# A fused attention and channel-mix kernel: the same tasks in another order and on other engines, with two planner prices changed

## The chip, the cores and the metric

The kernel runs on one core of one Trainium2 chip. A core has a tensor engine (PE in the profile; its weight loads are shown as PEld), a vector engine (DVE), a scalar engine (ACT), GpSimd (POOL) and a sync engine (SP), which here only issues DMAs. The metric is the device time of one execution in microseconds (us), lower is better. The kernel before took 271.17 us as the median of 4 runs (269.69 to 272.12).

## The reference, cut to what matters

Eight batches, eight heads, 576 positions, head size 64. Attention is causal by blocks of 64 positions, its output becomes a matrix of 576 rows by 512 columns for each batch, and this goes through a channel-mix layer with a shift by one position.

```python
mask = (pos[:, None] // 64) >= (pos[None, :] // 64)
attn = softmax(where(mask, q @ k.T / 8, -1e9))           # 8 batches x 8 heads, 576 x 576
x = (attn @ v) as (8, 576, 512)                          # heads side by side
x_prev = x shifted by one position, zeros in front       # inside each batch
xk = mu_k * x + (1 - mu_k) * x_prev                      # and xr with mu_r
k = relu(xk @ w_k)                                       # 512 -> 1024
out = sigmoid(xr @ w_r) * ((k * k) @ w_v)                # 1024 -> 512
```

## The kernel before

**Work and its units.** The kernel computes batch after batch of attention and feeds the result, as columns of a transposed `x`, into ten chunks of the channel mix: chunks 0 and 1 have 256 positions, chunks 2 to 9 have 512. Chunk c (2 to 8) begins in the columns of batch c - 2 and ends in those of batch c - 1, chunk 9 lies in batch 7; the two halves of the kernel overlap, one batch's attention with an earlier chunk's channel mix.

Everything is cut into tasks. Those on PE have names, which the string `TENSOR` lists in the order in which PE executes them:

- `qBPN`: transposes of queries or keys of head pair P (only batches 0 and 1; later batches use a transposing DMA, L534);
- `sBPI` (and `sBtQ`): scores of batch B, pair P, part I (L652, L660). An exponential on ACT (`ex`, L679) follows, and on POOL a memset of masked corners (`zero`, L688);
- `dBQ` (for batch 0 also `eBQ`): the softmax sums of half Q of the heads (L725), followed on DVE by reciprocals (L777, L780) and shuffles that spread them (L786);
- `vBQI`: probabilities times values (L725), followed on DVE by the **normalization** (`norm`, L822, L833 and L835): it multiplies the sums in PSUM by the spread reciprocals and writes `x` (tile `t_xt`). In L833 and L835 the operands are read in steps of four positions, since the scores are laid out by residues of 4;
- `kCJ`: chunk C, column block J of the first matrix (L958), followed on ACT by relu (L969) and by a square `sqCJ` on ACT (L976), or on DVE or POOL (L978);
- `rCJ`: the gate matrix (L993), followed by tanh on ACT (L1004);
- `pCJ`: the projection back (L1024, 8 matmuls), followed on DVE by the product with the gate (`ov`, L1036) and on SP by the output DMA (L1042);
- fills (L1062), two matmuls each without use, put in where PE would stand idle before the first `k`.

Between the normalization and `kCJ` stand, for each of four column blocks cc of a chunk: the difference `dCcc` on DVE or POOL (L907), and two `mul` on DVE (L920) that make `xk` and `xr`; where a batch begins inside a chunk, a small `fix` on POOL (L935) for each of the two. So `kC0` waits for the last `norm`, the last difference, four `mul` of `xk` and the `fix`.

**What sets the order.** Nothing is scheduled at run time. `Plan` is given the order on PE (`TENSOR`) and for 260 further tasks the engine (`WHERE`: casts of loaded tensors `qk`, `v`, `wk`, `wr`, `wv`, evacuations `ev`, squares `sq`, differences `d`). Each task has a price in microseconds. From the prices `dues` derives when each task off PE is due, and `order` goes through a planned time and takes on each engine the most urgent task whose inputs and buffers are free by the plan. What comes out is a fixed sequence for each engine. On the chip each engine executes its sequence in order and waits where an input is late, with all that stands behind it. SP issues its DMAs in order too: the loads, the transposing DMAs and the outputs are one queue. A price does not change an instruction; it changes the sequences.

The sequences also depend on ring buffers (`RINGS`): 4 PSUM buffers `mm` for all matmul outputs but scores, 2 PSUM buffers `s` for scores, 4 tiles `e` of probabilities, 9 load buffers `ld`, and so on.

Of the kernel before, what the change touches and what calls it, by code (L numbers as in the profile page):

```python
# [21 lines left out]


TENSOR = """
q000 q010 q001 q011 s000 q030 s010 s001 q110 q100 q020 s011 s012 s002 s0t0 d00
v000 q021 q031 e00 s020 s0t1 q130 s030 s032 v001 s022 v002 q120 s021 s031 q131
q111 q121 q101 v010 d01 s110 s100 s1t0 s112 v011 e01 v012 s1t1 s102 k00 s111
s101 s130 k03 s120 d10 k10 s132 s131 k14 k16 k02 k01 k12 s121 s122 v100 k05
k07 v101 k13 k17 k11 k04 k06 d11 v102 r00 v111 r10 r01 k15 s200 s202 v112 v110
s2t0 r11 s210 s212 p00 p01 p10 p11 r21 r23 k20 k26 k27 k24 r20 k25 k22 s211  # L30
s201 k21 k23 r22 s230 d20 s220 p23 s221 v201 s232 v200 s231 v202 s222 p20 s2t1
v210 s300 d21 s301 s302 v211 s310 p21 v212 s312 s3t0 p22 s311 s330 k30 k31 k37
s331 s332 k32 r33 d30 s320 k34 s322 k35 r32 s321 s3t1 k33 r31 k36 d31 v300
v312 p32 r30 v311 p33 v301 v302 v310 s400 s401 p31 s402 s410 p30 s411 s4t0 k40
k44 s412 s430 k45 r42 r41 k43 d40 s431 k46 r43 s420 s421 k47 k42 k41 r40 v400
v401 v402 s432 s422 p40 s4t1 p43 d41 v411 v410 s500 p41 p42 v412 s501 s502 k50
k53 s510 s5t0 k57 k56 s512 k52 k51 k54 s520 s511 r53 r51 s530 s532 d50 r52 k55
s5t1 v500 v501 r50 s531 s522 p51 v502 s521 s600 p52 d51 s602 s601 v512 v511
v510 p50 p53 s610 s612 k60 k65 s620 s611 k62 r60 r62 s6t0 s630 k66 k63 k64 d60
s632 s631 k61 k67 s622 r63 v600 v601 v602 s6t1 r61 s621 p60 p61 s700 s702 d61  # L40
v611 v610 v612 s701 s710 p63 s730 s731 p62 s711 s712 k70 k74 k77 s7t0 s732 k73
k72 r73 k76 r70 s7t1 s720 d70 v700 v701 s721 s722 k71 r71 k75 r72 v702 d71
v711 v710 p72 p71 p73 p70 v712 k80 k87 k86 k83 k82 r80 k84 k85 r83 k81 r82 r81
p80 p83 p82 p81 r90 k90 k92 k91 k96 k93 k94 k97 k95 r93 r92 p90 r91 p91 p92
p93b p93a
"""


WHERE = {
    "ACT": "ev000 ev001 ev011 ev021 ev030 ev101 ev111 ev120 ev121 ev130 qk0001 "  # L50
            "qk1011 qk220 qk221 qk230 qk231 qk301 qk310 qk320 qk321 qk400 qk401 "
            "qk521 qk530 qk531 qk611 qk621 qk630 qk631 qk711 qk720 qk721 qk730 "
            "qk731 sq02 sq04 sq07 sq12 sq14 sq15 sq23 sq31 sq32 sq35 sq36 sq40 "
            "sq42 sq43 sq45 sq50 sq52 sq55 sq66 sq71 sq75 sq80 sq81 sq84 sq86 "
            "sq87 sq91 sq93 sq96 v04 v11 v12 v14 v20 v21 v22 v23 v32 v40 v42 "
            "v43 v64 v70 v71 wk5 wr1 wv1 wv5 wv6 wv7",
    "DVE": "d00 d02 d13 d20 d21 d22 d30 d32 d33 d42 d51 d53 d62 d63 d71 d72 "
            "d73 d82 d83 d90 d91 d92 d93 ev010 ev020 ev031 ev100 ev110 ev131 "
            "qk0000 qk0101 qk0111 qk1000 qk1001 qk1101 qk200 qk210 qk211 qk311 "
            "qk330 qk331 qk410 qk411 qk431 qk600 qk601 qk700 qk701 qk710 sq00 "  # L60
            "sq03 sq13 sq20 sq24 sq26 sq27 sq33 sq44 sq47 sq51 sq53 sq60 sq61 "
            "sq62 sq70 sq73 sq77 sq82 sq83 sq85 sq94 sq95 sq97 v00 v01 v02 v24 "
            "v30 v33 v41 v50 v54 wk3 wk6 wk7 wr2 wv0 wv3",
    "POOL": "d01 d03 d10 d11 d12 d23 d31 d40 d41 d43 d50 d52 d60 d61 d70 d80 "
            "d81 qk0010 qk0011 qk0100 qk0110 qk1010 qk1100 qk1110 qk1111 qk201 "
            "qk300 qk420 qk421 qk430 qk500 qk501 qk510 qk511 qk520 qk610 qk620 "
            "sq01 sq05 sq06 sq10 sq11 sq16 sq17 sq21 sq22 sq25 sq30 sq34 sq37 "
            "sq41 sq46 sq54 sq56 sq57 sq63 sq64 sq65 sq67 sq72 sq74 sq76 sq90 "
            "sq92 v03 v10 v13 v31 v34 v44 v51 v52 v53 v60 v61 v62 v63 v72 v73 "
            "v74 wk0 wk1 wk2 wk4 wr0 wr3 wv2 wv4",  # L70
}


# [207 lines left out]
def kernel(  # L281
# [24 lines left out]
    M = CUT // J  # L306
# [73 lines left out]
    def flex(key, alts, fn, deps, takes=(), uses=(), lock=BOTH):  # L380


        eng = ENGINE.get(key, next(iter(alts)))
        t = plan.add(eng, alts[eng], lambda: fn(eng), deps, takes, uses,
                     lock=lock)
        t["key"], t["alts"] = key, alts
        return t
# [324 lines left out]
    def add_values(b, Q):  # L712
# [98 lines left out]
        def scale(t, i, xs, a, z, c, first, lo, hi, buf, rd, spr, key):  # L811
            home = HOME[c]
            take = not xt_parts[home]
            off = lo - CHUNKS[home][0]
            ch = slice(2 * Q + xs[0], 2 * Q + xs[-1] + 1)

            def norm():
                x = xt_tile(c)[:, ch, 1 + off:1 + off + hi - lo]
                num, r = tiles["num", b, Q, i], tiles["rd", key]
                n = len(xs)  # L820
                if a == M:
                    nc.vector.tensor_tensor(  # L822
                        x, num[:, 0:n * D].rearrange("p (s t) -> p s t", s=n),
                        r[:, J * MP:].unsqueeze(1).to_broadcast([P, n, D]),
                        ALU.mult)
                    return
                p0, p1 = (lo - b * S) // J, (hi - b * S) // J
                num = num[:, 0:n * J * (z - a)].rearrange(
                    "q (s j p) -> q s p j", s=n, j=J)[:, :, p0 - a:p1 - a]
                r = r[:, 0:J * MP].rearrange("q (j p) -> q p j", j=J)[:, p0:p1]  # L830
                x = x.rearrange("q s (p j) -> q s p j", j=J)
                if n == 1:
                    nc.vector.tensor_tensor(x[:, 0], num[:, 0], r, ALU.mult)  # L833
                else:
                    nc.vector.tensor_tensor(  # L835
                        x, num, r.unsqueeze(1).to_broadcast(
                            [P, n, p1 - p0, J]), ALU.mult)
            dur = 0.2 if a == M else 0.00105 * (hi - lo) * len(xs) + 0.065
            xb = xtbuf[home]
            n = on("DVE", dur, norm, [t, spr], takes=[xb] if take else [],  # L840
                   uses=[buf, rd] + ([] if take else [xb]))
            xt_parts[c].append(n)
            for x in xs:
                xt_of[c].setdefault(2 * Q + x, []).append(n)
# [17 lines left out]
    def xt_tile(c):  # L862
        c = HOME[c]
        if ("xt", c) not in tiles:
            tiles["xt", c] = new("xt", [P, CCn, CH + 1], FP)
            if c == 0:
                nc.vector.memset(tiles["xt", c][:, :, 0:1], 0.0)
        return tiles["xt", c]
# [22 lines left out]
    def add_mix(c, cc):  # L891
# [7 lines left out]
        f = W[c] / CH  # L899
# [4 lines left out]
        def fn(eng):  # L904
# [5 lines left out]
        sub = flex(f"d{c}{cc}", {usual: alts[usual], **alts}, fn,  # L910
                   list(xt_of[c][cc]), takes=[d], uses=[xtbuf[h]])
        for n in range(2):
            name = ("xk", "xr")[n]
            buf = tiles[name + "b", h]
            first = cc == 0 and h == c

            def mul(n=n, name=name, first=first):
                if first:
                    tiles[name, c] = new(name, [P, CCn, CH], F16)
                nc.vector.scalar_tensor_tensor(  # L920
                    tiles[name, h][:, cc, o:o + w], tiles["d", c, cc][:, 0:w],
                    (MUK1, MUR1)[n][:, cc:cc + 1],
                    xt_tile(c)[:, cc, o + 1:o + w + 1], ALU.mult, ALU.add)
            mixed[c, n].append(on(
                "DVE", 0.12 + 0.545 * f, mul, [sub] + mu_ready,
                takes=[buf] if first else [],
                uses=[d, xtbuf[h]] + ([] if first else [buf]), lock=BOTH))
            if cc < CCn - 1:
                continue

            for b in range(B):
                at = b * S - CHUNKS[c][0]
                if 0 < at < w:
                    def fix(n=n, at=at, name=name):
                        nc.gpsimd.tensor_tensor(  # L935
                            tiles[name, h][:, :, at:at + 1],
                            xt_tile(c)[:, :, at + 1:at + 2],
                            (MUK, MUR)[n][:, :].unsqueeze(2), ALU.mult)
                    mixed[c, n].append(on(
                        "POOL", 0.16, fix, list(mixed[c, n]),  # L940
                        uses=[buf, xtbuf[h]], lock=BOTH))
# [105 lines left out]
    mu_ready = []  # L1047
# [87 lines left out]
```

## Time and profile before

| | before |
|---|---|
| median of 4 runs | 271.17 us (269.69 to 272.12) |
| the profiled execution | 270.27 us |
| its span, first to last instruction | 268.5 us |
| PE busy | 250.1 us (93%) |
| DVE busy | 204.7 us (76%) |
| ACT busy | 197.3 us (73%) |
| POOL busy | 116.2 us (43%) |
| mean granted PE clock | 0.992 of full speed |
| `norm`, 128x448 (L833), 8 of them | mean 934 ns |
| `mul`, 128x512 (L920), 64 of them | mean 809 and 813 ns |
| difference 128x512 (L907) | DVE 712 ns, POOL 1075 ns |

The profiled execution is one run, on which all rows and stages below rest; its own time is 270.27 us, 0.9 us under the median. A busy share says how long an engine had an instruction in it. On DVE and ACT an instruction begins some 0.08 to 0.1 us before the one ahead of it ends, so that the mean duration in a row is more than what one more instruction costs; where this matters, the distance from start to start is used. First `k` of chunk c (L958) stood at 36.0, 40.7, 68.1, 97.0, 123.1, 150.2, 178.0, 206.1, 230.7 and 248.8 us for c = 0 to 9, and the first projection `p00` at 59.4 us.

### The profile page before, as it was taken

To read this page: it belongs to the slowest core of one execution; us is meant where nothing else is said; L and a number is where in the kernel's file an instruction comes from. 1 tells how busy PE (TensorE), PEld (TensorE's weight loads), DVE (VectorE), ACT (ScalarE), POOL (GpSimd) and SP (SyncE) were. 2 spreads that over 40 slices of the span, in tenths; PEclk is the share of its full clock that TensorE was granted. 3 is DMA by queue.
4 is the path that set the end of the run, shared out by engine and by line. 5 is a ranking of instruction groups with operands and counts; after the bars stand their busy time and mean duration, and the time that the engine had idled before them with its cause. 6 is when DMAs were issued, how large, how long until landed. Compare 5 with 4: busy or idle time off the path is not lost.

```text
span 268.5 us, 9965 instructions
## 1 busy us (share of the span) xinstructions
PE 250.1 (93%) x4120; PEld 131.0 (49%) x4120; DVE 204.7 (76%) x477; ACT 197.3 (73%) x313; POOL 116.2 (43%) x265
## 2 busy tenths in 40 slices
PE   0999799999999699999999899999999999999995
PEld 0667456654445344544455354534453455444443
DVE  2579987999529984799379938996799599996033
ACT  2769979996898679669992799759978880490740
POOL 3337737954054245644572396527652640000300
PEclk9999889999999999999999999999999999999999
DMA  7999899999998999999999999999994101302113
GB/s 226 305 275 248 241 276 291 251 218 224 249 200 236 180 186 244 262 190 234 276 223 209 185 310 183 166 202 301 228 187 130 59 2 42 120 0 96 64 39 117
DMA packets 118302, 51.51 MB, mean 192 GB/s; under 512 B 102769, under 2 KB 109169, under 8 KB 118257
## 3 DMA queue, kind: packets, MB, share of 16 engines
q1 hardware_dynamic: 118256, 50.88, 86.0%
q8 instruction: 32, 0.52, 0.8%
q14 instruction: 14, 0.11, 0.1%
HBM read 33.56 MB, written 9.44 MB: 160 GB/s over the span
## 4 chain that ended last, share of the span: by engine, by line
PE 69%; DVE 13%; ACT 9%; DMA 5%; issue 2%; SPq 0%; POOL 0%; DVEq 0%; ACTq 0%
PE t_mm L958 23%; PE t_mm L1024 16%; PE t_mm L993 12%; PE t_mm L725 10%; ACT t_e L679 7%; PE t_s L652 6%; DVE t_xt L833 3%; DMA t_qkt<-NB 3%; DVE t_xk L920 2%; PE t_s L660 2%; DMA t_ld<-in_k_dram 2%; DVE t_d L907 2%; DVE t_rd L786 2%; DVE t_c L777 1%; DVE t_o L1036 1%
## 5 line engine op out<-in xcount | busy, mean ns | idle before, releaser
L679 ACT ACTIVATE t_e<-t_s 128x1024 f16<-128x1024 f32 x96 | 95.6, 1032 | 23.4 <-PE t_s L652 12.8
L958 PE MATMUL t_mm<-t_xk,WK 128*128 128x512 f16 (+1 forms) x320 | 68.9, 359 | 2.8 <-DVE t_xt L833 1.7
L1024 PE MATMUL t_mm<-WV,t_k 128*128 128x512 f16 (+1 forms) x296 | 66.0, 374 | 0.0
L969 ACT ACTIVATE t_kr<-t_mm 128x512 f32<-128x512 f32 (+1 forms) x80 | 43.9, 576 | 13.3 <-PE t_mm L958 13.0
L688 POOL MEMSET t_e<- 64x128 f16 x128 | 24.4, 208 | 57.0 <-ACT t_e L679 54.8
L958 PEld LDWEIGHTS <-WK 128*128 128x128 f16 x320 | 29.0, 98 | 33.5 <-issue 3.6
L1024 PEld LDWEIGHTS <-t_k 128*128 128x128 f16 x296 | 27.4, 98 | 31.8 <-issue 2.4
L652 PE MATMUL t_s<-t_qkt 64*128 64x128 bf16 (+3 forms) x272 | 35.9, 326 | 4.9 <-DMA t_qkt<-NB 2.9
L978 POOL TENSOR_TENSOR t_k<-t_kr 128x512 f16<-128x512 f32 (+1 forms) x27 | 26.2, 977 | 28.5 <-ACT t_kr L969 28.4
L993 PE MATMUL t_mm<-WR,t_xr 128*128 128x512 f16 x144 | 35.9, 380 | 0.0
L833 DVE TENSOR_TENSOR t_xt<-t_mm,t_rd 128x448 f32<-128x448 f32 (+6 forms) x56 | 30.7, 595 | 4.4 <-PE t_mm L725 4.0
L1004 ACT ACTIVATE t_t<-t_mm 128x512 f32<-128x512 f32 x36 | 21.8, 615 | 14.5 <-PE t_mm L993 14.3
L777 DVE RECIPROCAL t_c<-t_mm 128x128 f32<-128x128 f32 (+1 forms) x18 | 15.6, 865 | 20.8 <-PE t_mm L725 20.7
L1036 DVE SCALAR_TENSOR_TENSOR t_o<-t_t,t_mm 128x512 f32<-128x512 f32 (+1 forms) x37 | 24.4, 668 | 8.5 <-PE t_mm L1024 7.9
L920 DVE SCALAR_TENSOR_TENSOR t_xk<-t_d,MUK,t_xt 128x512 f16<-128x512 f32 (+1 forms) x40 | 29.5, 764 | 1.0 <-POOL t_d L907 0.9
L725 PE MATMUL t_mm<-t_e,VO 128*32 128x64 f16 (+4 forms) x1056 | 29.5, 252 | 0.2 <-DVE t_qkt L398 0.2
L920 DVE SCALAR_TENSOR_TENSOR t_xr<-t_d,MUR,t_xt 128x512 f16<-128x512 f32 (+1 forms) x40 | 29.2, 757 | 0.0
L978 DVE TENSOR_TENSOR t_k<-t_kr 128x512 f16<-128x512 f32 (+1 forms) x24 | 17.0, 723 | 15.4 <-ACT t_kr L969 15.1
L725 PEld LDWEIGHTS <-VO 128*32 128x32 f16 x1184 | 19.6, 99 | 10.6 <-issue 4.1
L660 PE MATMUL t_s<-t_qkt 64*128 64x64 bf16 x320 | 23.9, 197 | 0.6 <-ACT t_e L679 0.5
L652 PEld LDWEIGHTS <-t_qkt 64*128 64x128 bf16 x272 | 13.3, 96 | 17.5 <-issue 8.9
L993 PEld LDWEIGHTS <-t_xr 128*128 128x128 f16 x144 | 13.4, 98 | 16.1 <-issue 0.5
(61 smaller groups left out, 281.7 us busy)
## 6 DMA issues: line engine op xcount, KB each, us to landing
out_dram<-t_o SPq DMA_DIRECT2D x35, 256.0 KB, 3.5
t_vl<-in_v_dram SPq DMA_DIRECT2D x32, 256.0 KB, 5.6
t_ld<-in_k_dram SPq DMA_DIRECT2D x48, 128.0 KB, 4.2
t_ld<-in_q_dram SPq DMA_DIRECT2D x24, 256.0 KB, 4.1
t_ld<-in_q_dram SPq DMA_DIRECT2D x8, 288.0 KB, 5.7
t_ld<-in_k_dram SPq DMA_DIRECT2D x8, 288.0 KB, 5.1
t_ld<-in_moe_w_k_dram SPq DMA_DIRECT2D x8, 256.0 KB, 4.4
t_ld<-in_moe_w_v_dram SPq DMA_DIRECT2D x8, 256.0 KB, 3.9
```

The lines of the kernel that those rows point to most:

```text
L652: nc.tensor.matmul(PS[:, h, col:col + J * w].rearrange("p (j n) -> p j n", j=J), keys, ask[:, 0:CUT].rearrange("d (p j) -> d j p" if b < T ...
L660: nc.tensor.matmul(PS[:, h, col:col + D], keys, ask[:, CUT:S], start=True, stop=True)
L679: nc.scalar.activation(tiles["e", b, pr][:, :, i, :], tiles["ps", b, pr, i], AF.Exp, scale=ISQ)
L725: nc.tensor.matmul(ps[g * R:g * R + R], lhs, e, start=start, stop=stop, tile_position=(0, g * R))
L833: nc.vector.tensor_tensor(x[:, 0], num[:, 0], r, ALU.mult)
L920: nc.vector.scalar_tensor_tensor(tiles[name, h][:, cc, o:o + w], tiles["d", c, cc][:, 0:w], (MUK1, MUR1)[n][:, cc:cc + 1], xt_tile(c)[:, c ...
L958: nc.tensor.matmul(ps[:, 0:w], WK[:, cc, jc * P:(jc + 1) * P], tiles["xk", h][:, cc, o:o + w], start=(cc == 0), stop=(cc == CCn - 1))
L969: nc.scalar.activation(tiles["kr", c, jc][:, 0:w], tiles["pk", c, jc][:, 0:w], AF.Relu)
L978: (nc.vector if eng == "DVE" else nc.gpsimd).tensor_tensor(K2, KR, KR, ALU.mult)
L993: nc.tensor.matmul(ps, tiles["xr", h][:, cc, o + jt * P:o + (jt + 1) * P], WR[:, cc], start=(cc == 0), stop=(cc == CCn - 1))
L1024: nc.tensor.matmul(ps[:, 0:w], tiles["k2", h][:, jc, off:off + P], WV[:, jc, cols], start=(jc == 0), stop=(jc == JCn - 1))
L1036: nc.vector.scalar_tensor_tensor(tiles["o", c, jt, part][:, 0:w], tiles["t", c, jt][:, cols], 1.0, tiles["pv", c, jt, part][:, 0:w], ALU.a ...
```

## The change

Three things are replaced together.

1. Two prices in the planner. The normalization's price goes from 0.00105 to 0.00174 us for each column and head (plus 0.065 us), and the price of a `mul` from 0.12 + 0.545 f to 0.14 + 0.525 f, where f is the chunk's share of 512 columns (so 0.665 both before and after for a full chunk, and 0.3925 against 0.4025 for a half one).
2. `TENSOR`: the same task names in another order.
3. `WHERE`: 166 of 260 tasks go to another engine. By kind, before and after, as DVE / ACT / POOL: differences 23/0/17 and 16/0/24; squares 24/29/27 and 29/25/26; casts of queries and keys 20/24/20 and 18/24/22; casts of values 9/15/16 and 12/14/14; casts of the first matrix 3/1/4 and 1/2/5, of the gate matrix 1/1/2 and 0/2/2, of the last matrix 2/4/2 and 3/4/1; evacuations 6/10/0 both.

No other instruction is added or removed, but for the fills: the plan puts in 16 before and 12 after.

```diff
 TENSOR = """
-q000 q010 q001 q011 s000 q030 s010 s001 q110 q100 q020 s011 s012 s002 s0t0 d00
-v000 q021 q031 e00 s020 s0t1 q130 s030 s032 v001 s022 v002 q120 s021 s031 q131
-q111 q121 q101 v010 d01 s110 s100 s1t0 s112 v011 e01 v012 s1t1 s102 k00 s111
...
-r33 d30 s320 k34 s322 k35 r32 s321 s3t1 k33 r31 k36 d31 v300
-v312 p32 r30 v311 p33 v301 v302 v310 s400 s401 p31 s402 s410 p30 s411 s4t0 k40
...
-v400
-v401 v402 s432 s422 p40 s4t1 p43 d41 v411 v410 s500 p41 p42 v412 s501 s502 k50
-k53 s510 s5t0 k57 k56 s512 k52 k51 k54 s520 s511 r53 r51 s530 s532 d50 r52 k55
-s5t1 v500 v501 r50 s531 s522 p51 v502 s521 s600 p52 d51 s602 s601 v512 v511
-v510 p50 p53 s610 s612 k60
...
+q000 q001 q011 q010 s000 s010 q031 s001 s011 q020 q021 q030 d00 v000 s012 s030
+q100 q110 s002 s020 s0t0 s021 s032 d01 q101 v010 s0t1 e00 s031 v001 v002 s022
+s100 q111 s101 k00 k02 k01 s110 q120 s111 e01 v011 v012 q131 s112 s1t0 q130
...
+s3t1 p31 d31 s400 s402 p33 v312 v311 v310 p30 p32 s401 k40
...
+p41 s421 s422 p40 s4t1 v401 d41 s500 s501 p43 v411 v410 s5t0 s510 v412
+s512 s502 p42 s511 s530 k50
...
+r51 d51 v511 v510 s601 s602 v512
+p50 s610 s6t0 p51 p53 s620 s611 p52 s630 s612 k60
...
 WHERE = {
-    "DVE": "... d82 d83 d90 d91 d92 d93 ..."
+    "POOL": "... d80 d81 d82 d83 d90 d91 d92 d93 ..."
...
-            dur = 0.2 if a == M else 0.00105 * (hi - lo) * len(xs) + 0.065
+            dur = 0.2 if a == M else 0.00174 * (hi - lo) * len(xs) + 0.065
...
-                "DVE", 0.12 + 0.545 * f, mul, [sub] + mu_ready,
+                "DVE", 0.14 + 0.525 * f, mul, [sub] + mu_ready,
```

## The prediction

> **What bounds the kernel now.** I read the page's busy shares first, then stages, then what PE waited for, then the start-up on ACT.
>
> ```profile
> PE 250.1 (93%) x4120; PEld 131.0 (49%) x4120; DVE 204.7 (76%) x477; ACT 197.3 (73%) x313; POOL 116.2 (43%) x265
> ...
> PE 69%; DVE 13%; ACT 9%; DMA 5%; issue 2%; SPq 0%; POOL 0%; DVEq 0%; ACTq 0%
> ```
>
> The second line is the chain that ended last: 69% is PE, the rest is where PE stood behind DVE, ACT or a DMA. The change leaves PE's work as it is, so it can win back only such time. Stages (busy us of PE, PEld, DVE, ACT, POOL, each with its instructions, then clock, DMA share and GB/s):
>
> ```profile
> 10.00:40.00 30.00, 27.43 (x700) 18.90 (x699) 25.68 (x78) 24.73 (x34) 16.28 (x42) 0.94 0.99 261
> 68.00:97.00 29.00, 26.49 (x473) 12.95 (x471) 21.49 (x51) 23.80 (x36) 9.59 (x26) 1.00 1.06 215
> 150.00:178.00 28.00, 27.32 (x474) 13.44 (x474) 22.16 (x53) 22.70 (x35) 16.36 (x38) 1.00 1.18 217
> 230.60:268.50 37.90, 34.73 (x168) 16.38 (x168) 20.64 (x35) 17.76 (x32) 2.25 (x3) 0.99 0.20 77
> ```
>
> The middle runs at 98% of PE with about half a microsecond lost per chunk, the end at 100% but for the last output. PE's own waits, in us in total, times, longest:
>
> ```profile
> PE t_s L652 <- DMA t_qkt<-NB: 2.9, 2, 2.5
> PE t_mm L958 <- DVE t_xt L833: 1.7, 2, 1.2
> PE t_s L652 <- ACT t_e L679: 1.4, 3, 0.7
> PE t_mm L958 <- DVE t_o L1036: 0.4, 1, 0.4
> ```
>
> After 60 us PE's gaps are 2.51 (at 91.64, `s310` behind its transposing DMA), 1.22 (150.19, `k50`), 0.52 (178.03, `k60`), 0.36 (203.03, a DMA again) and 0.39 (230.67, `k80`): **5.0 us** that an order can remove. Before 60 us ACT sets the pace; its idle times there are in brackets:
>
> ```profile
> 18.82 0.64 ACT L392 COPY t_qkt<-t_mm 128x576 bf16<-128x576 bf16 x1 [1.27 <-PE t_mm L470]
> 20.77 1.02 ACT L679 ACTIVATE t_e<-t_s 128x1024 f16<-128x1024 f32 x1 [1.31 <-PE t_s L660]
> 35.67 0.38 ACT L667 ACTIVATE EL<-t_s 64x256 f16<-64x256 f32 x1 [1.58 <-PE t_s L660]
> ```
>
> That is **4.2 us** of idle time of the engine that sets the pace.
>
> **Is the new price right?** Four normalizations in a row on DVE, 448, 64, 448 and 64 columns:
>
> ```profile
> 217.35 2.14 DVE L833 TENSOR_TENSOR t_xt<-t_mm,t_rd 128x448 f32<-128x448 f32 x4
> ```
>
> The old price gives 2 x (0.535 + 0.132) = 1.33 us, the new one 2 x (0.845 + 0.176) = 2.04. The old plan therefore saw 0.00069 x 2048 = 1.4 us too little DVE work for each batch (512 columns, 2 halves, 2 heads, twice). It is missing on the way from a chunk's last `dB1` to its `kC0`, and it shows in who releases PE: not the `mul` that makes `xk`, but a `norm` (L833). At `k50` the last `mul` had ended at 149.63 and a `norm` for the next chunk ran from 149.56 to 150.13: `k50` takes the fourth-last PSUM buffer `mm`, which that `norm` had yet to read. At `k60` it is the same (`mul` 177.27, `norm` until 177.89, PE at 178.03), at `k80` an `ov` (230.62). So a way is covered when PE has enough other tasks for DVE's whole series, those `norm`s and `ov`s included.
>
> **The change part by part.**
>
> *Cover of the critical way.* Projections (1.73 us each, "1.73 PE t_mm L1024 x8" in the chain) that stand between the last `dB1` and the chunk's first `k`, read from `TENSOR`, chunks 3 to 8: before 2, 4, 2, 2, 2, 4; after 3, 3, 2, 4, 3 and 4, and for chunk 7 two `r` besides, for chunk 8 an `r` and a `k` (0.86 each). Sum 16 before, 19 after. I went through each way with start-to-start distances (reciprocals 1.3, shuffles 4 x 0.21, `norm` 0.85 for 448 columns, difference 0.60 on DVE and 1.05 on POOL, `mul` 0.66, `ov` 0.60). `k60`: PE 10.8 us, DVE 7.5: covered. `k40`: 7.8 against 8.1, its buffer waits for a `norm` behind the `mul`s. `k30`: 7.4 against 7.4, with POOL's `fix` last. `k50`: 7.8 against 8.0, since the `fix` on POOL stands behind the `zero` of `s502`. `k70` 12.0 against 11.5, `k80` 11.1 against 10.6. I leave 1.1 us for these together, against 2.1 before.
>
> *Transposing DMAs.* Before, `s310` follows `s302`, `v211` directly after `d21`, and waited 2.51. After, three projections, three `k` and an `r` come between (8 us). The tightest one becomes `s430`: its casts sit on DVE behind four `ov`, about 10.5 us behind `d31`, its DMA needs up to 7.5 (84.14 to 91.64 in the chain), and PE arrives after 18.3. I leave 0.9 for all, against 2.9. Both together: 5.0 to 2.0, **-3.0 us** (bounds: -5.0, and +2 if the new order has waits as large as before in more places).
>
> *Start-up.* The keys of heads 4 to 7 stood behind four other loads and two of values; their cast on POOL began at 13.42 and 18.32. After, they are loads 5 and 6, right behind the first four, and all four loads of this half land before batch 1's. So `s030`, `s020` come before ACT runs dry, and ACT has chunk 0's relus early (`k00 k02 k01` before `s110`) for the gap at 35.67. Against that, by row means ACT has 55.6 us of work ahead of `p00`, 54.2 before. I take 3.0 of the 4.2 us, less 1.4: **-1.6 us** (bounds -4.2 to +1.4). The cover for this is DVE, which has 4 us less ahead of `p00` (46.5 against 50.6 by row means).
>
> *PE from `p00` on.* One projection is already done (`p11`), and `s210`, `s212`, `s2t0`, `v112` less `s201` come later: -1.73 + 0.43 + 0.20 + 0.42 = **-0.7 us**. Changes of mode on PE: 119 against 120, nothing.
>
> *Engines.* By row means DVE loses 2.9 us in all, ACT 1.5, POOL gains 5.4. Net seven differences go from DVE to POOL (of the 512-wide, POOL has 12 before and 20 after). Each is 0.45 us longer there, and meets a `mul`:
>
> ```profile
> 220.11 1.21 POOL L907 TENSOR_TENSOR t_d<-t_xt 128x512 f32<-128x512 f32 x1
> ...
> 220.34 1.53 DVE L920 SCALAR_TENSOR_TENSOR t_xr<-t_d,MUR,t_xt 128x512 f16<-128x512 f32 x1
> ```
>
> A `mul` is 0.745 us in the median and 1.34 to 1.53 in 5 of 64, 4 of which met a difference on POOL. 4 in 12 then becomes some 7 in 20: three more, 0.7 us each, 2.1 us of DVE, half of it on the way to a `k`: **+1.0 us** (0 to 2.1 more per three meetings).
>
> The Trainium skill speaks against this move: "SBUF — State Buffer", section "SBUF: two separate sides", says that the port pair which DVE and GpSimd share is an exclusive lock, and an operation with two SBUF inputs on DVE blocks for the whole of a GpSimd one. By that rule every meeting costs up to 1.05 us, where the rows show 0.6 to 0.8, and as an estimate by that page a meeting for each of the eight more would make +8 us on DVE. The rows agree that it blocks, and show that only one difference in three meets.
>
> *The end.* From `k80` on both orders have the same 32 tasks on PE, 34.8 us. After, seven squares of chunk 8 are on ACT (10 us of relus, squares and tanh against 10.4 us of PE until `p83`): nothing, and 0.5 if it is late. Differences of chunk 9 on POOL are hidden by the 19 us until `r92`.
>
> Sum: -3.0 - 1.6 - 0.7 + 1.0 = -4.3. The profiled execution's 270.27 becomes 266.0; its time lies 0.9 under the median, so I forecast **266.9 us** as a median.
>
> **Rivals.**
>
> *The gains are not of the order's making (no change).* The correction itself can return only what waits for DVE, 1.22 + 0.52 + 0.39 = 2.1 us; the DMA wait and the start-up depend on landings that no plan knows. If the start-up gives nothing and a DMA is late once elsewhere for 2.5, there remain -2.1 + 1.0 - 0.7 + 0.5: 269.9 as a median. For it: the planner's DMA and latency prices are unchanged. Against it: the load order in the first 10 us is plain. Chance 0.24.
>
> *POOL's queue takes DVE's place (slower).* POOL goes from 116 to about 121 us, and executes in order: `fix`, which a chunk's first `k` needs, stands behind `zero`s that wait for ACT's exponentials, and behind the moved differences. Place: `k30` to `k80`, where all margins but that of `k60` are between -0.3 and +0.5. If each chain is 1.5 us longer (two more meetings of 0.7), six chunks lose 9 us less some 1.5 of margin: 270.27 + 0.9 - 4.3 + 7.5 = 274.4. It decides from about 0.9 us per chunk on. Against it: POOL is idle over half the time in all stages. Chance 0.18.
>
> *Start-up at its best.* All 4.2 us less 1.4, and every wait gone: 270.27 + 0.9 - 5.0 - 2.8 - 0.7 + 0.5 = 263.2. Part of my own case.
>
> **How the numbers follow.** Forecast's case 0.58, no change 0.24, slower 0.18. A measurement of this kernel tells about 1% from no change: below 268.5 is faster, above 273.9 slower. The range reaches from the best start-up, 263.2, to within the slower case, 272.5.
>
> **What the profile will show.** Right: no idle of over 1 us on ACT between 15 and 30 us; `p00` near 57.8; `k20` near 65; no wait of PE of over 1 us after 60; steps from `kC0` to the next near 26 to 27; from `k80` to the end 37.8 as before. Wrong: PE waiting for POOL's `fix` or difference in front of `k50`, `k70`, `k80`; more than 8 `mul` over 1.2 us; ACT idle in front of `s100`; a transposing DMA that lands after `s430` or `s420` was due.

## The result and the profile after

| | before | after |
|---|---|---|
| median | 271.29 us (57 runs) | 269.60 us (38 runs) |
| ratio to before | 1 | 0.9939, 95% interval 0.9922 to 0.9957 |
| the profiled execution, its span | 270.27, 268.5 us | 270.31, 268.5 us |
| first matmul | 6.48 us | 7.96 us |
| `p00`, first `k` of chunk 2 | 59.4, 68.1 us | 61.0, 67.6 us |
| first `k` of chunks 3 to 8 | 97.0, 123.1, 150.2, 178.0, 206.1, 230.7 | 94.8, 122.3, 152.4, 180.1, 208.6, 230.7 |

The change gains 1.7 us, 0.6% (1.2 to 2.1 us by the interval); the forecast was 266.9 us, a gain of 4.3. That is inside the range. The medians take all runs, the ratios here and below leave out those more than 1.5% above the fastest of the same kernel. The two profiled executions are equally long and do not show the gain: the one of the new kernel lies 0.7 us above its median, the one of before 1.0 under. So no stage is judged here from this pair alone; the experiments below give more executions of the same sequences.

Busy time and the chain that ended last, from the page of the new kernel:

```profile
PE 247.8 (92%) x4112; PEld 129.7 (48%) x4112; DVE 204.8 (76%) x474; ACT 195.7 (73%) x310; POOL 124.0 (46%) x271
...
PE 55%; ACT 16%; DMA 11%; DVE 7%; issue 5%; POOL 2%; SPq 2%; POOLq 0%; ACTq 0%; DVEq 0%
```

Of the busy times ACT's came as expected (-1.6 us for -1.5). DVE was to lose 2.9 us and stayed the same, and POOL gained 7.8 for 5.4; part of that is in the port meetings below. In the chain DVE's share fell from 13 to 7%, and ACT's rose from 9 to 16, DMA's from 5 to 11. The same stages as before, in the same columns:

```profile
10.00:40.00 30.00, 25.95 (x691) 18.37 (x689) 24.11 (x73) 27.31 (x42) 17.13 (x44) 0.94 0.99 248
68.00:97.00 29.00, 27.98 (x460) 13.76 (x459) 20.63 (x53) 21.44 (x34) 13.28 (x28) 1.00 1.05 209
150.00:178.00 28.00, 26.97 (x466) 13.23 (x465) 26.19 (x59) 22.93 (x37) 12.70 (x32) 1.00 1.10 220
230.60:268.50 37.90, 34.84 (x192) 16.45 (x176) 20.06 (x28) 18.14 (x33) 8.64 (x8) 1.00 0.20 77
```

From 10 to 40 us ACT is now busy 27.3 of 30 us (24.7 before), the stage from 68 to 97 us has 1.5 us more of PE, and the end is as it was. PE's own waits after 68 us, in us in total, times, longest:

```profile
PE t_s L660 <- ACT t_e L679: 0.9, 1, 0.9
PE t_s L652 <- DMA t_qkt<-NB: 0.6, 1, 0.6
PE t_s L652 <- ACT t_e L679: 0.6, 2, 0.4
PE t_s L652 <- ACT EL L667: 0.6, 1, 0.6
PE t_mm L1024 <- DVE t_xt L833: 0.3, 1, 0.3
PE t_mm L958 <- POOL t_xk L935: 0.3, 1, 0.3
PE t_mm L958 <- DVE t_xt L833: 0.2, 1, 0.2
PE t_mm L725 <- POOL t_e L688: 0.2, 1, 0.2
```

Before, the same view had three rows: 2.9 for a DMA, 1.7 and 0.4 for DVE, 5.0 us in all. Now it is 3.7. The old waits are nearly gone (1.1 left of 5.0), but 2.1 us wait for ACT and 0.5 for POOL, which had none. ACT's timeline between 15 and 40 us, the rows with an idle time (in brackets, as before):

```profile
15.41 0.64 ACT L392 COPY t_qkt<-t_mm 128x576 bf16<-128x576 bf16 x1 [0.32 <-PE t_mm L470]
17.75 3.77 ACT L679 ACTIVATE t_e<-t_s 128x1024 f16<-128x1024 f32 x4 [0.25 <-PE t_s L660]
27.03 1.03 ACT L679 ACTIVATE t_e<-t_s 128x1024 f16<-128x1024 f32 x1 [0.52 <-PE t_s L652]
28.96 1.94 ACT L679 ACTIVATE t_e<-t_s 128x1024 f16<-128x1024 f32 x2 [0.34 <-PE t_s L660]
38.97 0.62 ACT L392 CAST WK<-t_ld 128x512 f16<-128x512 f32 x1 [0.27 <-DMA t_ld<-in_moe_w_k_dram]
```

The three gaps of 4.2 us are gone, 1.7 us in small ones are left.

### The profile page after: what moved, and what is told of

The parts are those of the page before. It is cut to its first block, busy times and chain, and to the rows that moved or that the text cites. A ratio compares the mean times of both kernels' runs of the same rounds, so it can differ in the third digit from the quotient of the medians.

```text
span 268.5 us, 9966 instructions
## 1 busy us (share of the span) xinstructions
PE 247.8 (92%) x4112; PEld 129.7 (48%) x4112; DVE 204.8 (76%) x474; ACT 195.7 (73%) x310; POOL 124.0 (46%) x271
## 4 chain that ended last, share of the span: by engine, by line
PE 55%; ACT 16%; DMA 11%; DVE 7%; issue 5%; POOL 2%; SPq 2%; POOLq 0%; ACTq 0%; DVEq 0%
PE t_mm L1024 19%; PE t_mm L958 12%; PE t_mm L725 8%; PE t_mm L993 8%; ACT t_e L679 7%; DMA t_ld<-in_q_dram 5%; PE t_s L652 5%; DMA t_qkt<-NB 4%; ACT t_kr L969 4%; ACT t_t L1004 2%; DMA t_ld<-in_moe_w_k_dram 2%; SPq L373 2%; PE t_s L660 2%; PE t_mm L470 2%; ACT NB L392 1%
## 5 line engine op out<-in xcount | busy, mean ns | idle before, releaser
L969 ACT ACTIVATE t_kr<-t_mm 128x512 f32<-128x512 f32 (+1 forms) x80 | 42.9, 567 | 20.0 <-PE t_mm L958 19.6
L688 POOL MEMSET t_e<- 64x128 f16 x128 | 24.7, 210 | 58.0 <-ACT t_e L679 55.8
L958 PEld LDWEIGHTS <-WK 128*128 128x128 f16 x320 | 29.6, 98 | 31.6 <-issue 2.2
L1024 PEld LDWEIGHTS <-t_k 128*128 128x128 f16 x296 | 27.2, 98 | 32.1 <-issue 2.1
L652 PE MATMUL t_s<-t_qkt 64*128 64x256 bf16 (+3 forms) x272 | 35.2, 327 | 3.4 <-ACT t_e L679 2.0
L978 POOL TENSOR_TENSOR t_k<-t_kr 128x512 f16<-128x512 f32 (+1 forms) x26 | 24.9, 965 | 26.9 <-ACT t_kr L969 26.7
L907 POOL TENSOR_TENSOR t_d<-t_xt 128x512 f32<-128x512 f32 (+1 forms) x24 | 25.4, 1065 | 12.9 <-DVE t_xt L833 12.6
L920 DVE SCALAR_TENSOR_TENSOR t_xr<-t_d,MUR,t_xt 128x512 f16<-128x512 f32 (+1 forms) x40 | 31.4, 807 | 0.0
L978 DVE TENSOR_TENSOR t_k<-t_kr 128x512 f16<-128x512 f32 (+1 forms) x29 | 20.9, 732 | 10.8 <-ACT t_kr L969 10.4
L725 PE MATMUL t_mm<-t_e,VO 128*32 128x64 f16 (+4 forms) x1056 | 27.5, 248 | 0.7 <-issue 0.7
L725 PEld LDWEIGHTS <-VO 128*32 128x32 f16 x1184 | 18.9, 97 | 10.5 <-issue 6.0
```

The source lines that it names most:

```text
L652: nc.tensor.matmul(PS[:, h, col:col + J * w].rearrange("p (j n) -> p j n", j=J), keys, ask[:, 0:CUT].rearrange("d (p j) -> d j p" if b < T ...
L725: nc.tensor.matmul(ps[g * R:g * R + R], lhs, e, start=start, stop=stop, tile_position=(0, g * R))
L920: nc.vector.scalar_tensor_tensor(tiles[name, h][:, cc, o:o + w], tiles["d", c, cc][:, 0:w], (MUK1, MUR1)[n][:, cc:cc + 1], xt_tile(c)[:, c ...
L958: nc.tensor.matmul(ps[:, 0:w], WK[:, cc, jc * P:(jc + 1) * P], tiles["xk", h][:, cc, o:o + w], start=(cc == 0), stop=(cc == CCn - 1))
L969: nc.scalar.activation(tiles["kr", c, jc][:, 0:w], tiles["pk", c, jc][:, 0:w], AF.Relu)
L978: (nc.vector if eng == "DVE" else nc.gpsimd).tensor_tensor(K2, KR, KR, ALU.mult)
```

## Experiments

### Parts of the change, planned anew

Four kernels keep the planner. Three splice the two orders of `TENSOR` at a task, or a few tasks from it (what the first order has listed is left out of the second) and take each `WHERE` key from the order that holds its task; one changes the prices alone. In e1 to e3 and e5 lines are one higher than in the two kernels, in e4 two.

```diff
 e1: TENSOR, WHERE: before's up to k20, after's from there; prices new
 e2: TENSOR, WHERE: after's up to k20, before's from there; prices new
 e3: TENSOR, WHERE: after's, but between k40 and k50 before's; prices new
 e4: TENSOR, WHERE as before:
-            dur = 0.2 if a == M else 0.00105 * (hi - lo) * len(xs) + 0.065
+            dur = 0.2 if a == M else 0.00174 * (hi - lo) * len(xs) + 0.065
...
-                "DVE", 0.12 + 0.545 * f, mul, [sub] + mu_ready,
+                "DVE", 0.14 + 0.525 * f, mul, [sub] + mu_ready,
```

> The old order and division up to the first k20 (68 us), the new ones after it; new prices. Theory: the start-up returned nothing and the new steady state carries the gain of 1.7 us, so this one keeps it: ratio to before 0.993 to 0.995. Rival 1, the start-up carries it, and the late first loads of the profiled run (7.11 against 5.74 us) hid that: 0.999 to 1.001. Rival 2, the new start-up costs time by itself (1.5 us more between PE's work and the clock at k20, 25.2 against 23.7): 0.988 to 0.990.

> The mirror image: the new order and division up to k20, the old ones after it; new prices. Theory (the start-up returned nothing): ratio 0.999 to 1.001. Rival 1 (the start-up carries the gain): 0.993 to 0.995. Rival 2 (the new start-up costs 1.4 us): 1.004 to 1.006.

> The new kernel with the old order and division between k40 and k50 alone, where the profiled runs show the new order 1.5 us behind (PE waits 0.93 and 0.43 us for ACT's exponentials and 0.28 for POOL's fix). Theory: the loss belongs to this stretch's order, and comes again in every run: ratio to before 0.988 to 0.990. Rival: it is chance of one run, or what is won here is lost at the next stage: 0.993 to 0.995, as the new kernel.

> The kernel before with the two new prices alone: same TENSOR, same WHERE, only the sequences of the flexible tasks on ACT, DVE, POOL and SP shift (42 to 58 tasks on DVE, POOL and ACT). Theory: which engine does what and PE's order carry the gain, and the price only served to find them: ratio 0.998 to 1.002. Rival: the sequences by truer due times carry it: 0.993 to 0.995.

All four are slower than both kernels: 1.0224 (1.0173 to 1.0275), 1.0165 (1.0107 to 1.0223), 1.0266 (1.0213 to 1.0320) and 1.0245 (1.0183 to 1.0307). Neither theory nor rival of any of the four had that. The splices do not keep the old sequences on either side of the cut: planned anew, ACT, DVE, POOL and SP get other sequences, and new waits appear far from the cut. PE's waits after 68 us come to 7.5, 9.2, 10.0 and 7.6 us in e1 to e4, against 5.0 in the kernel before. In e2, whose order on PE behind `k20` is the old one, it is POOL's `fix`, in front of `k30` to `k60`; in e4, where only prices differ, it is exponentials on ACT (2.5 us in three waits) and the `fix` in front of `k50` (1.5). PE's waits in e2 (us in total, times, longest):

```profile
PE t_mm L959 <- POOL t_xk L936: 6.8, 4, 2.5
```

PE's timeline in e4:

```profile
121.83 0.28 PE L654 MATMUL t_s<-t_qkt 64*128 64x256 bf16 x2 [1.70 <-ACT t_e L681]
```

The first is the very mechanism of the slower rival, POOL's queue: in front of `k50` the `fix` stands behind `zero`s that wait for exponentials. The second is longer than any wait that the change removes but one. The mirror of e4 came later: the new order planned with the old prices.

> The new kernel planned with the old prices of the normalization and the mul: same TENSOR and WHERE, the sequences of 33 to 45 tasks on ACT, DVE and POOL shift. Theory: an order fits only the sequences that it was planned with, whether the price is true or not; as the old order lost 2.45% by the new prices, this one loses by the old ones: 1.010 to 1.025. Rival: the true price is what makes the sequences good, and an order planned with it stands small shifts: 0.994 to 1.002.

It took 1.0105 (1.0023 to 1.0187), at the lower end of what the theory said. This rests on two of its four runs; by the medians of all (276.11 against 270.72 us) it is 1.020, and the rival is out either way. One wait for a transposing DMA between `k40` and `k50`, 4.5 us, stands out in its profile. So, in the two orders tried, **an order fits the sequences that it was planned with**: the old one loses 2.45% by the truer price, the new one about 1.7% by the old price. The truer price alone did not help; whether it was what found the better plan is not shown.

### Sequences written out

To change one stretch without moving the rest, the sequences of all five engines were taken from the two plans and written into the kernel as one list; both plans have the same 1395 tasks, so that a list may change over from one to the other at a task.

```diff
-    for t in plan.order(TENSOR.split()):
-        t["fn"]()
+    for n in ORDER.split():
+        (plan.fills.pop() if n == "f" else plan.tasks[int(n)])["fn"]()
...
+ORDER = """ (numbers of the tasks) """
 f1: after's list up to k20, then before's     f2: before's up to k20, then after's
 f3: after's up to p23, before's up to s602, then after's
 f4: before's; 13 tasks moved in front of p23 (not the mirror image of f3)
```

> No planning any more: the sequences of all five engines are written out as the plan gave them for the two kernels, so that a stretch can be changed without moving the others. Here the new kernel's sequences and division up to the first k20, the old kernel's from there. Theory (ledger of clock less PE's work in the two profiled runs: start-up +1.5 of which 1.4 is a late first load, k20 to k30 -2.2, k30 to k40 +0.9, k40 to k50 +1.5, k50 to k80 -1.2): the start-up gives nothing, ratio to before 0.998 to 1.002. Rival (the start-up carries the gain, as p00 at 58.37 in the run with the old stretch from k40 to k50 suggests): 0.988 to 0.994.

> The mirror image, sequences written out: the old ones up to k20, the new ones from there. Theory (start-up gives nothing, the steady state carries all): 0.992 to 0.996. Rival (the start-up carries it, and the steady state gives nothing): 0.999 to 1.004.

f1: 0.9963 (0.9930 to 0.9995). f2: 1.0021 (0.9989 to 1.0052). Against 0.9939 for the whole, the new start-up alone is worth 1.0 us, and the new steady state another 0.7 behind the new start-up, but -0.6 behind the old one; each of these is uncertain by some 0.9 us. The parts do not add up: PE's waits after 68 us come to 5.3 us in both, as in the kernel before (5.0), and in f2 two of them are at places where the new kernel has a smaller one or none (1.3 for a copy on POOL, 1.0 for `EL`). So only rough bounds follow: the front carries 1.0 to 2.2 us of the gain, the rest lies between 0.7 gained and 0.6 lost. The theory that the steady state carries all is wrong, since f2's interval lies above its range; that the start-up gives nothing is unlikely, f1's interval ends just under 1.

> Sequences written out: new up to p23 (84 us, so with the new start-up and without the old wait for a transposing DMA in front of k30), old from there up to s602 (168 us: the old k30 to k50, without the new order's waits of PE for ACT's exponentials at 142 and 149 us), new from there to the end. Theory: the ledger's stages are properties of the order, the new kernel loses 0.9 + 1.5 us there, so this one is 2.4 us faster than the new kernel: ratio to before 0.983 to 0.988. Rival (the stages' differences are chance of single runs): 0.993 to 1.000.

> The mirror image of the one before: old up to p23, new up to s602, old to the end. Theory: it has the old DMA wait and the new waits for exponentials, and is slower than both: ratio to before 1.006 to 1.012. Rival (chance): 0.994 to 1.002.

f3: 1.0238 (1.0183 to 1.0294). f4: 1.0211 (1.0164 to 1.0258). The f4 that ran is not what was expected of it: its `WHERE` is the old one throughout, and its list is before's but for 13 tasks that stand in front of `p23`. Among these are five loads of batch 3's values and one of batch 4's queries, and behind them the transposing DMA that `s310` needs. So nothing was measured of the mirror image, but f4 shows what one transposing DMA costs behind six loads. In both kernels one stretch, `k20` to `k30`, holds the loss. PE's waits in f3:

```profile
PE t_s L652 <- DMA t_qkt<-NB: 5.5, 1, 5.5
```

and in f4:

```profile
PE t_s L652 <- DMA t_qkt<-NB: 6.1, 1, 6.1
```

It is `s310`. SP's timeline in the kernel before and, the last two rows, in f4:

```profile
84.14 3.30 SPq L534 DMA_TRANSPOSE t_qkt<-NB  x1
...
84.55 5.71 SPq L373 DMA_DIRECT2D t_vl<-in_v_dram  x4
...
92.14 3.30 SPq L534 DMA_TRANSPOSE t_qkt<-NB  x2
```

In f3 the loads of values come ahead of it too, and SP reaches it at 90.05. The stretch takes 36.0 us in f3 against 27.2 in the new kernel, and 35.8 in f4 against 28.9 in the kernel before, so the loss is 8.8 and 6.9 us, more than the longer wait (5.5 and 3.6). Most of the rest is PE's clock, see the last section. So f3 says little on its question, and f4 did not ask it, but they show the price of a transposing DMA out of place: 5.5 to 6.1 us at once, and a half clock beside it.

### Single waits taken away

f5 moves one cast, f6 seven, f7 two; the rest of the new kernel's list stays.

```diff
 f5, f6: qk520     ACT -> POOL, in front of the tail cast of batch 5, pair 2
 f6:     qk420 qk700 v70     ACT -> POOL       qk510 qk530 v64     DVE -> POOL
 f7:     wr0 wr3 on ACT: behind relu of k05, k14, k11 in place of in front
```

> The new kernel's sequences written out, with one task moved: the cast qk520 (the queries of heads 4 and 5 of batch 5), for whose load ACT stands idle 1.79 us (138.67 to 140.46) with two exponentials queued behind it, goes to POOL, which is idle there. Theory: the new order's loss between k40 and k50 comes from casts that wait for a load in ACT's queue; PE's waits of 0.93 us at 142.06 and 0.18 at 143.23 go: ratio to before 0.988 to 0.991, against 0.994 for the new kernel. Rival: the next wait (exponentials at 149.38, POOL's fix at 152.43) takes it up: 0.993 to 0.995.

> As the run with one cast, and six more casts that wait for a DMA on ACT or DVE after 60 us in the new kernel go to POOL: qk420, qk700, v70 from ACT (1.54, 1.30, 1.81 us idle in front of them), qk510, qk530, v64 from DVE (0.76, 2.37, 1.55). Theory: ACT and DVE then wait for DMAs about 0.7 and 0 us after 60 us in place of 7.1 and 4.7, and most of PE's remaining 3.8 us of waits go: 0.982 to 0.988. Rival: POOL's zeros and fixes wait behind the same DMAs and PE waits for those: 0.994 to 1.004.

> The new kernel's sequences written out, with ACT's two casts of w_r (each waits 0.20 to 0.25 us for its load at 42 to 44 us) behind the three relus that follow them. Theory (start-up): PE's wait of 0.89 us for a PSUM buffer at 44.41 goes, p11 and all that follows come 0.6 to 0.9 us earlier: 0.990 to 0.992. Rival: from 44 to 61 us ACT's exponentials set the pace, which the change leaves as they were: 0.993 to 0.996.

f5: 0.9926 (0.9884 to 0.9969), f6: 0.9950 (0.9909 to 0.9991), f7: 0.9982 (0.9951 to 1.0014). f5 and f6 do not differ from the new kernel (0.9939) by more than the intervals; f7 is, if anything, slower. In f6 the waits of ACT and DVE for DMAs after 68 us are gone, from 7.1 and 4.7 us to 0.7 and 0. PE's waits in f6 after 68 us:

```profile
PE t_s L652 <- DMA t_qkt<-NB: 0.8, 1, 0.8
PE t_mm L958 <- POOL t_xk L935: 0.8, 1, 0.8
PE t_s L652 <- ACT t_e L679: 0.6, 2, 0.4
PE t_s L652 <- ACT EL L667: 0.6, 1, 0.6
...
```

With three rows for DVE of 0.8 together that is 3.6 us, against 3.7. The wait of 0.93 for an exponential is gone, and so it is in f7 and f9, where that cast was not touched: it was chance of one execution. The others are the order's own. They stand at the same places in f5, f6 and f7 (2.7 us in all in f7): 0.59 for `EL` at 80 to 84 us, 0.43 for an exponential at 146 to 149, and at `k50` POOL's `fix`, 0.41 to 0.80. So the theory that casts behind late loads eat the gain is wrong, and f5's rival "the next wait takes it up" fits better.

### What was still open

```diff
 f8: after's list up to s0t0 (20 us), then before's     f9: the mirror image
 f10: before's list, the last 4 of its 16 fills left out
 f11: after's up to s322, before's up to s602, then after's
```

> Sequences written out: the new ones up to s0t0 (some 20 us: the new order of the first loads, keys of heads 4 to 7 as loads 5 and 6, s030 and s020 earlier), the old ones from there. Theory (the start-up's gain is the earlier keys, which fill ACT's idle time at 18 to 21 us): ratio to before 0.992 to 0.996. Rival (the gain is in the order of the weights, relus and projections between 20 us and k20): 0.999 to 1.002.

> The mirror image: old sequences up to s0t0, new ones from there. Theory (earlier keys carry the gain): 0.999 to 1.002. Rival: 0.993 to 0.996.

> The old kernel's sequences with the last four of its 16 fills left out (the new kernel has 12; fills are matmuls whose result nothing reads, so the output is whole). Theory: they lie in PE's idle time and cost and give nothing: ratio 0.998 to 1.002. Rival: they cost their 0.11 us each (0.998) or hold up the granted clock, and without them PE is slower before 40 us (1.002 to 1.005). PE's waits behind 68 us in its profile: 5.2 again if the one profile of the old kernel was typical, 3 to 4 if the transposing DMA's 2.5 us were chance.

> Sequences written out: new up to s322 (behind k30 and the scores s310 to s321, so that the transposing DMAs keep their places in SP's queue), old from there up to s602 (168 us), new from there on. Theory: the new order loses 0.9 between k30 and k40 and 0.6 to 1.0 between k40 and k50 against the old one, so this one is up to 1.5 us faster than the new kernel: ratio to before 0.986 to 0.991. Rival: each cut costs as much as the stretch gains (the two cuts at k20 cost 1.2 us together): 0.992 to 0.997.

f8: 1.0268 (1.0221 to 1.0315). One wait again, in PE's timeline, for a transpose of batch 1:

```profile
29.72 0.47 PE L470 MATMUL t_mm<-identb,t_nl 64*128 64x64 bf16 x6 [8.21 <-DVE t_nl L398]
```

In the chain of f8 its load was issued at 23.15, behind the loads of four blocks of `w_k`; the new order loads these weights first and asks for batch 1's second half later, the old one the other way round. So the order of loads and PE's order belong together, and whether the early keys carry the start-up's gain cannot be told by this cut; that stays open. f9, with 1.0004 (0.9961 to 1.0046) and a similar wait of 2.07 us at 25.31, does not tell either.

f10: 1.0022 (0.9992 to 1.0053), so the four fills cost nothing that can be seen; whether leaving them out loses up to 1.4 us, as the rival has it, is not settled. Its waits after 68 us are those of the old kernel, in a second execution:

```profile
PE t_s L652 <- DMA t_qkt<-NB: 2.6, 1, 2.6
PE t_mm L958 <- DVE t_xt L833: 2.2, 3, 1.2
PE t_mm L958 <- DVE t_o L1036: 0.4, 1, 0.4
```

So the prediction's 5.0 us of removable waits were no chance. f11: 1.0094 (1.0057 to 1.0132). It has `k40` to `k50` in 27.1 us like the old kernel (new: 30.1), but around the cut PE waits 0.9 us for an exponential and 1.7 for POOL's `zero`, and at the next one 1.5 for exponentials. No mixture beat the new kernel beyond its interval.

## Why the prediction came out as it did

**Direction and range right, size wrong: 1.7 us for 4.3.** Eight executions share the new sequences up to `p00` (after, e2, e3, f1, f3, f5, f6, f11; in e2 a few `mul` of chunk 2 change places) and four the old ones (before, f2, f4, f10), so each step has more than one reading.

*Cover of the critical way and DMAs, -3.0: this is the step that failed.* PE's waits after 68 us were to fall from 5.0 to 2.0. They fell to 3.7, so the term is -1.3 and not -3.0 (3.4, 3.6, 2.7 and 3.8 in f5, f6, f7 and f9; 5.2 in f10 for the old order). What the step named did happen: the DMA wait in front of `k30` (2.51, in f10 2.59) and DVE's at `k50` (1.22, in f10 1.22) went, and what is left for DVE and DMAs is 1.1, less than the 2.0 granted. What the step put at nothing is when ACT frees the two score buffers `s`. Each way was weighed by DVE's series and PE's cover; the new order issues scores where ACT has not yet read the last ones, and that gives 2.1 us of new waits (1.2 where the chance one is left out). `k50` came as feared: POOL's `fix` is last, 0.3 to 0.8 us late.

*Start-up, -1.6: too much by 1.0.* ACT's idle time shrank as said, 4.2 to 1.7 us. But `p00` comes at 59.28 us in the mean of eight (58.37 to 60.98) against 59.83 of four (59.42 to 60.10): -0.6, not -1.6. Two things were left out or too small. ACT is busy 49.3 to 49.8 us ahead of `p00` in three of the new (after, f1, f5) and 47.4 and 47.7 in two of the old (before, f10): 1.6 to 2.5 more by busy time, where the sum had 1.4 by row means. And a wait on POOL was not foreseen. In the chain of the profiled execution (start, us, what):

```profile
30.22 5.54 DMA t_ld<-in_moe_w_k_dram
...
35.88 0.61 POOL WK L398
...
38.74 0.76 POOL t_d L907
```

A load of `w_k` lands at 35.76; POOL has stood idle for it 1.3 us, then casts two blocks of weights and two of values before it comes to the difference that chunk 1's last `xk` needs. It is the rival's mechanism, POOL's queue, in the start-up instead of `k30` to `k80`. Of the eight only f6 has this wait too (1.9 us), and these two have the latest `p00`, 60.98 and 60.05; the other six, with 0.3 or less, have 58.37 to 59.32, in the mean 58.87, a gain of 1.0. f7, which took another wait out of this stretch, gained nothing.

*PE from `p00` on, -0.7: right.* From `p00` to `k20` it is 6.63 us in the new sequences and 8.64 to 8.87 in the old (f2 apart, where `s201` stands in between): -2.1, of which 1.3 are only moved (`r21`, `r23`, 1.73, now follow `k20`, `s201`, 0.43, stands before `p00`). That leaves -0.8. With the start-up's -0.6 it makes -1.4 for the front, in line with f1's 1.0.

*Port meetings, +1.0: did not come where it counts.* Before 230 us 2 `mul` take over 1.2 us, 5 before the change; POOL has the eight more 512-wide differences, but six of them belong to chunks 8 and 9. There they do meet, four `mul` take over 1.2 us, and the two engines slow each other: in DVE's timeline four `mul` of `xr`,

```profile
236.28 5.08 DVE L920 SCALAR_TENSOR_TENSOR t_xr<-t_d,MUR,t_xt 128x512 f16<-128x512 f32 x4
```

and in POOL's the differences beside them:

```profile
235.76 4.38 POOL L907 TENSOR_TENSOR t_d<-t_xt 128x512 f32<-128x512 f32 x3
```

The first three of these `mul` take 1.52 us and each difference 1.48 (0.74 and 1.04 alone, in rows close by). This fits the exclusive lock between DVE and GpSimd that the Trainium skill states ("SBUF — State Buffer", section "SBUF: two separate sides"), and both engines show it. But `r92`, the first task that reads the result, comes only at 248.0 us. The rate of "one meeting in three" was carried over to differences in another place, where nothing waits.

*The end.* 34.7 us from `k80` to PE's last matmul, as before: right.

**The sum.** The predicted steps split at `k20` into -2.3 for the front and -2.0 for the rest; f1 and f2 have -1.0 to -2.2 and -0.7 to +0.6, by their middles. The front holds, at its lower part; the rest is what is missing. In the profiles the rest gains more than that. With the 1.3 us that were only moved taken off, `k20` to `k80` took 160.3 to 162.0 us in after, f5, f6, f7 and f9, against 162.6 in before and 164.2 in f10 (of whose difference the clock makes 1.6, see the last section). Why front and rest by the profiles (-1.4 and at least -0.6) come to more than the 1.7 of the medians is open. One thing was not tried: in f5 to f7 the mean granted clock of the runs was 0.987 to 0.989, against 0.993 in the 29 runs of before beside them; in f1, f2 and f9 it was no lower.

**Rivals.** "No change" had the time almost to the point (269.9), by luck: it had a DMA late once elsewhere and no gain in the start-up, but the DMA wait went and stayed away, the front gained, and it is ACT, not a DMA, that took the place. The slower rival did not come true in this kernel, but e2 shows its mechanism at work, 6.8 us in four waits.

## What to carry to other kernels

When an order is changed to cover one engine's series, go through every other producer that PE's next task needs in the same way, above all who frees its buffers: here the waits named were nearly all removed, 3.9 us, and 2.6 came back on other engines. Where all queues are planned as a whole, order, loads and division are one object; parts of two good plans put together lost up to 2.7% (f1 and f2 lost least), and a truer price alone lost 2.45%. A single profiled execution may lie a per cent from the median (e4: 276.46 against 279.69 us), so stages are best compared over several kernels that share a stretch.

## What was not expected of the hardware

The first three loads stand in the same order in all kernels, but the third one landed between 5.1 and 7.1 us after the start, and with it the first matmul began between 5.95 and 7.96 us; the profiled run of the new kernel had the latest of all. In the mean it is 7.2 us for eleven kernels with the new first tasks and 6.8 for seven with the old. Some 0.1 of the 0.4 is the change's: from landing to matmul it is 0.85 us where the first cast of that load is on POOL, 0.75 where it is on ACT. How much of it reaches `p00` is open: f1 and f11 began at 5.95 and 7.62 and had it at 58.74 and 59.05, f4 and f2 at 6.16 and 7.62, with 60.00 and 59.81.

A long wait of PE can cost more than its length. The granted clock falls to half for 3.4 us or a multiple of it. From 60 us to the end of PE's work ten of the 18 profiled executions have one such stretch, and in each it begins during a wait of PE of 1.5 us or more, or within 2 us of its end (f10 2.6, f3 5.5, f4 6.1 us); after, f1, f2, f5, f6, f7 and f9 have no wait over 1.4 us there, and no such stretch. Not every wait has one: before, with 2.5, has none. So before and f10 show the price; PE behind `s310` in before, in f10, and f10's stage (columns as above, the clock third from the end):

```profile
91.96 1.90 PE L1024 MATMUL t_mm<-WV,t_k 128*128 128x512 f16 x8
...
92.94 3.15 PE L1024 MATMUL t_mm<-WV,t_k 128*128 128x512 f16 x8
...
93.40:96.80 3.40, 3.40 (x49) 1.38 (x49) 3.40 (x7) 1.70 (x3) 1.07 (x3) 0.50 0.96 156
```

`k20` to `k30` takes 28.9 us in before and 30.5 in f10, with the same wait. In f3 and f4 the clock is at half for 6.8 and 10.2 us.

Waits in the steady state mostly come back to the hundredth: `k50`'s wait for DVE was 1.20 to 1.23 us in before, f1, f3, f4, f8, f10 and f11, that for `EL` 0.58 to 0.59 in after, f3, f5, f6, f7, f9 and f11, but 1.02 in f2, and that for POOL's `fix` at `k50` lay between 0.28 and 0.80. A second execution tells an order's own wait from chance.
